# Clamped maxima go to their row in one transfer: strided query tiles, a split first hash and a new instruction list

## The chip, the cores and the metric

The kernel runs on 1 core of one Trainium2 chip. The metric is the device time of one execution in microseconds (us); lower is better. Three runs of the kernel before gave 386.69, 387.50 and 391.12 us, a median of 387.5 us.

## What is computed

Attention in which a query sees only the keys of its own hash bucket, and then a mixture-of-experts layer on the 128 best tokens of each batch. There are 4 batches of 8 heads (32 heads), 768 tokens and 64 numbers per head.

```python
def _attn_ref(q, k, v, proj):                       # q, k, v: 4 x 8 x 768 x 64; proj: 64 x 6
    q_bits = (einsum('bhsd,dk->bhsk', q, proj) > 0)   # 6 sign bits make a bucket
    k_bits = (einsum('bhsd,dk->bhsk', k, proj) > 0)
    mask = q_bucket[:, :, :, None] == k_bucket[:, :, None, :]
    scores = where(mask, scale * q @ k.T, -1e9)
    scores = scores - max(scores, axis=-1)            # one maximum for each query
    attn = exp(scores); attn = attn / (sum(attn, axis=-1) + 1e-9)
    return attn @ v

def _moe_ref(x, w_gate, w1, w2, capacity=128):      # x: 4 x 768 x 512, the heads side by side
    for b in range(4):
        top_idx = the 128 tokens with the highest x[b] @ w_gate
        xe = x[b, top_idx]; ye = relu(xe @ w1) @ w2   # w1: 512 x 1024, w2: 1024 x 512
        out[b, top_idx] = xe + sigmoid(scores[top_idx])[:, None] * ye
```

## The kernel before

**Data of a head.** For each head `h`, `A[h % 5]` is a tile of 97 partitions by 2 by 768 numbers in f16. Slot 0 holds the queries and slot 1 the keys, one column per token. Partitions 0 to 63 are the numbers of the head, 64 to 81 are rows of signs made from the hash (they push the score of a pair from different buckets far down), and partition 96 (`MROW`) holds, in slot 0, each query's clamped maximum, which the matmul with the keys' row of constants then subtracts. `Bt[h % 4]` holds the same numbers in another arrangement, with the low-order rests of the f32 inputs (`XL`), and is added in a second matmul.

**The work of a head, by the words of the list.** `X` loads queries and keys, `xh` (ScalarE) and `xl` (GpSimd) split them in f16 parts, `h` and `sg` make the signs for four heads at once, and `pa`, `ps`, `pb` are transfers that put these parts into `A` and `Bt`. Then comes a first pass for the maximum. `kd` subtracts two thirds of the keys from their neighbours; `mx.h.g.s` (`max_unit`, L538) multiplies the query tiles of a group with a third of the keys: group 0 has four query tiles of 128, group 1 has two, and there are three steps `s`, so 18 matmuls of 256 columns and 18 weight loads a head, whose stationary operand is `a[0:KM, 0, t * P : (t + 1) * P]`, tile `t` being 128 neighbouring queries. Between two steps `re` (ScalarE, L546) applies a relu in place. `rd` (VectorE, L554) reduces over the keys, which leaves `m`, 128 partitions by 6: partition `p`, column `t` is the maximum of query `t * 128 + p`.

**From the maxima to the row.** For heads 2 to 31 four words follow: `mq` (`max_clamp`, L562, VectorE) writes the clamped and scaled maxima into the first 6 columns of a tile of 128 by 128; `mt` (`max_turn`, L566, TensorE) transposes that tile into a PSUM tile; `mc` (`max_copy`, L570, VectorE) copies its 6 partitions by 128 into `mr`; and `mr` (`max_row`, L575) starts, on SyncE's queue, the transfer of `mr` to partition 96 of `A`. Heads 0 and 1 (`ROWS`) take another way (`mk`, `mu`, `mv`), with small matmuls straight to partition 96.

**After the row.** `s.h.u` (`st_unit`, L624 and L627) computes scores for five units of a head, `e` (ScalarE, L640) exponentiates, `r` (VectorE, L654) takes the rests, `a.h.c` (`av`, L708) multiplies with the values, 18 matmuls of 64 or 65 columns for a chunk of 128 keys, and `rc`, `n`, `po` divide and put out. The words `sc`, `tp`, `ty`, `ts`, `sb`, `lt`, `ow`, `cl`, `cw`, `se`, `ip`, `ix`, `ga` rank and gather the tokens of a batch, `up`, `hh`, `hl`, `dn`, `fi` are the two layers (L963, L994), and `sr` scatters the result.

**The start.** Head 0 is hashed directly from its f32 input, in two halves of 384 tokens: `hx.0.0` and `hx.0.1` (`hash_direct`, L338, TensorE) write columns 0 to 383 and 512 to 895 of one PSUM tile of 1024 columns (`big`), and `sx.0.i.e` (`signs_direct`, L349, VectorE) turns half `e` into the signs of slot `i`. `dd.0.0.0` and `da.0.1.0` (L363, L360) copy rows of the input to `A[0]`, and `da.0.0.1`, `da.0.1.1` copy them to `Bt[0]` on ScalarE. `wa.k.n` are n matmuls without use for the result.

**What sets the order.** A list of words written out by hand or by a planner (`ORDER`) is executed word by word, and each engine and each queue takes its own instructions in that order. `BANKS` gives, for each PSUM tile in the order of the list, which of four slots it takes (three of 1024 columns, one of 512). Waits between engines follow from tiles that are written and read.

Of the kernel before, what the change touches and what calls it, by code (L numbers as in the profile page):

```python
# [10 lines left out]
F16 = mybir.dt.float16  # L11
# [8 lines left out]
P = 128  # L20
# [29 lines left out]
X.5 s.0.0 mx.1.0.2 vw.0 zb ws.0 xl.3 e.0.0 wc.0 rd.1.0 mx.1.1.2 rd.1.1 s.0.2 pp xh.6 w.0 mk.1.1 ps.2.0 mk.1.0 pb.1.1  # L50
kd.2 X.4 pa.3.1 ps.3.1 e.0.2 r.0.0 s.0.1 e.0.1 r.0.1 ia.3 X.7 s.0.3 e.0.3 xh.5 vs.1 ps.3.0 mu.1.0 mv.1.0 xl.6 pb.2.3
s.0.4 V.2 a.0.0 pb.2.2 a.0.1 a.0.2 e.0.4 mu.1.1 xh.4 mx.2.1.0 mv.1.1 re.2.1.0 mx.2.0.0 pb.3.3 pa.3.0 pa.5.1 s.1.3
re.2.0.0 kd.3 mx.2.1.1 ia.4 e.1.3 a.0.3 ia.2 mx.2.0.1 re.2.0.1 re.2.1.1 s.1.4 e.1.4 r.0.2 s.1.0 e.1.0 xl.5 xh.7
mx.2.0.2 xl.4 X.8 pa.4.0 mx.2.1.2 rd.2.0 rd.2.1 mq.2 pa.4.1 a.0.4 a.0.5 s.1.2 pb.2.0 rc.0 mt.2 e.1.2 mc.2 pb.2.1
pa.5.0 X.10 n.0 s.1.1 mx.3.0.0 e.1.1 w.1 mr.2 pb.5.2 mx.3.1.0 re.3.1.0 xl.7 pb.3.0 pa.6.0 h.1.0.4 r.1.0 a.1.0 r.1.1
a.1.1 a.1.2 re.3.0.0 mx.3.0.1 a.1.3 pb.4.3 vh.1 xh.8 re.3.0.1 pb.3.2 vw.1 sg.1.0.4 r.1.2 a.1.4 vr.1 ws.1 wc.1 mx.3.1.1
a.1.5 re.3.1.1 vl.1 vs.2 xh.10 rc.1 n.1 s.2.0 e.2.0 xl.8 wt.0 mx.3.0.2 vw.2 w.2 ps.4.1 ps.4.0 ps.5.1 s.2.2 X.11
mx.3.1.2 rd.3.0 ps.5.0 rd.3.1 mq.3 e.2.2 r.2.0 s.2.1 e.2.1 s.2.3 ps.6.1 e.2.3 V.3 pb.3.1 mt.3 mc.3 s.2.4 ws.2 wc.2
e.2.4 a.2.0 pa.6.1 kd.4 mx.4.0.0 r.2.1 mr.3 X.12 ps.6.0 re.4.0.0 ps.7.0 X.9 mx.4.1.0 re.4.1.0 kd.5 pb.6.2 a.2.1 r.2.2
# [141 lines left out]
def body(ctx, tc, qk, v, pj, wg, w1, w2, cst, cst16, out):  # L201
# [84 lines left out]
    def init_rest():  # L286
# [4 lines left out]
        for i in range(2):  # L291
            nc.gpsimd.memset(wide(f"mqi{i}"), 0.0)
# [40 lines left out]
    def hash_direct(h, e):  # L333
        if e == 0:
            st["hx", h] = big(f"hx{h}")
# [728 lines left out]
```

## Time and profile before

| | us |
|---|---|
| median of 3 runs | 387.5 |
| the profiled execution | 388.95 |
| its span from first to last instruction | 387.2 |
| TensorE busy in the span | 372.9 (96%) |
| ScalarE busy | 305.1 (79%) |
| VectorE busy | 301.7 (78%) |
| GpSimd busy | 138.8 (36%) |

Busy time is the union of an engine's instructions. The matmuls of TensorE overlap in their pipeline, so that one matmul lasts longer than the interval after which the next one starts; intervals between starts tell what a matmul costs.

### The profile page before, as it was taken

Reading aid. Unit: us, or ns where it says so; the run is one execution under the profiler, and the core shown is the slowest. Engines: PE = TensorE matmul, PEld = TensorE weight load, DVE = VectorE, ACT = ScalarE, POOL = GpSimd, SP = SyncE. Lnnn points to the kernel's source line nnn. Section 1 sums busy time; section 2 is a strip of 40 time slices with the busy share of each in tenths; the row PEclk is TensorE's granted clock in tenths of the full one; section 3 lists DMA queues with packets and bytes.
Section 4 is the critical chain, followed back from the end, with each engine's and each line's share of the span. In section 5 each row is a group of like instructions: output and inputs, shape, how many; then the busy total and the mean of one; then the engine's idle time right before and its main releaser. Section 6 shows DMA issues by size and latency. Waiting matters only on the chain.

```text
span 387.2 us, 13730 instructions
## 1 busy us (share of the span) xinstructions
PE 372.9 (96%) x5730; PEld 285.5 (74%) x5730; DVE 301.7 (78%) x666; ACT 305.1 (79%) x416; POOL 138.8 (36%) x157
## 2 busy tenths in 40 slices
PE   6899998999999999999999999999999999999994
PEld 4366877776777787878788886677787788797771
DVE  3686967887879999987987977859789989767521
ACT  4699999989998899999988788887788888651110
POOL 4777567258344246255432150436010200000021
PEclk9899999999999999999999999999999999999998
DMA  7477569676674566664555545333424514002110
GB/s 214 125 217 216 168 206 266 211 190 180 180 237 145 144 169 189 176 199 154 161 172 148 175 117 160 92 83 92 97 71 117 156 48 136 2 3 84 29 56 27
DMA packets 33850, 54.33 MB, mean 140 GB/s; under 512 B 5443, under 2 KB 25137, under 8 KB 33788
## 3 DMA queue, kind: packets, MB, share of 16 engines
q1 hardware_dynamic: 32908, 50.96, 45.5%
q0 software_dynamic: 640, 2.10, 1.7%
q8 instruction: 45, 0.74, 0.8%
q10 hardware_dynamic: 240, 0.39, 0.4%
q14 instruction: 17, 0.14, 0.1%
HBM read 26.04 MB, written 7.35 MB: 86 GB/s over the span
## 4 chain that ended last, share of the span: by engine, by line
PE 77%; ACT 8%; DVE 6%; issue 5%; DMA 2%; POOLq 0%; SPq 0%; DVEq 0%; ACTq 0%
PE av L708 23%; PE s L624 14%; PE s L627 14%; PE mx L538 13%; PE hp L963 4%; PE yp L994 4%; ACT mx L546 3%; ACT P L640 3%; PE h L380 2%; DVE R L654 1%; DVE m L554 1%; DMA X<-in_qk_dram 1%; DMA out_dram<-xe,idx 1%; DVE sg L393 1%; ACT V L462 1%
## 5 line engine op out<-in xcount | busy, mean ns | idle before, releaser
L640 ACT ACTIVATE P<-s 128x1024 int32<-128x1024 f32 (+1 forms) x160 | 145.5, 942 | 22.6 <-PE s L627 21.1
L624 PE MATMUL s<-A 97*128 97x256 f16 (+1 forms) x384 | 118.4, 326 | 1.1 <-DVE mr L570 0.3
L708 PEld LDWEIGHTS <-P 128*128 128x128 f16 x2304 | 115.3, 97 | 5.5 <-issue 0.3
L708 PE MATMUL av<-V,P 128*128 128x65 f16 (+1 forms) x2304 | 119.3, 193 | 0.0
L627 PE MATMUL s<-B 128*128 128x256 f16 (+1 forms) x384 | 117.9, 326 | 0.0
L708 PE MATMUL av<-VR,R 128*128 128x65 f16 x1152 | 115.6, 192 | 0.1
L546 ACT ACTIVATE mx<-mx 128x512 f32<-128x512 f32 (+2 forms) x127 | 99.4, 802 | 16.0 <-PE mx L538 12.1
L708 PEld LDWEIGHTS <-R 128*128 128x128 f16 x1152 | 105.2, 98 | 0.2 <-DVE R L654 0.2
L654 DVE TENSOR_SCALAR R<-P 128x1536 f16<-128x1536 uint16 x96 | 94.8, 999 | 9.4 <-ACT P L640 9.3
L412 POOL TENSOR_TENSOR XL<-X,XH 128x768 f16<-128x768 f32 x31 | 50.9, 1644 | 72.2 <-DMA A<-mr 17.6
L554 DVE TENSOR_REDUCE m<-mx 128x2 f32<-128x512 f32 (+1 forms) x65 | 60.6, 952 | 15.7 <-PE mx L538 15.0
L538 PEld LDWEIGHTS <-A 82*128 82x128 f16 x570 | 50.5, 97 | 22.0 <-issue 6.6
L538 PE MATMUL mx<-kd,A 82*128 82x256 f16 (+1 forms) x378 | 59.1, 273 | 1.4 <-DVE kd L512 0.5
L627 PEld LDWEIGHTS <-B 128*128 128x128 f16 x384 | 37.6, 98 | 20.7 <-issue 2.4
L624 PEld LDWEIGHTS <-A 97*128 97x128 f16 x384 | 37.4, 97 | 19.1 <-issue 0.8
L876 POOL DMA_INDIRECT xe<-out_dram,idx x4 | 6.5, 1628 | 79.6 <-DVE idx L871 79.4
L538 PE MATMUL mx<-A 82*128 82x256 f16 (+1 forms) x192 | 31.0, 273 | 1.3 <-ACT mx L546 0.9
L401 ACT CAST XH<-X 128x768 f16<-128x768 f32 x32 | 26.7, 839 | 2.3 <-DMA X<-in_qk_dram 2.2
L483 POOL TENSOR_TENSOR vs<-Vf 128x384 f32<-128x384 f32 x16 | 16.9, 1053 | 28.6 <-DMA Vf<-in_v_dram 28.5
L963 PE MATMUL hp<-xth,w1l 128*128 128x128 f16 x128 | 22.2, 219 | 0.0
L963 PE MATMUL hp<-xtl,w1h 128*128 128x128 f16 x128 | 22.2, 219 | 0.0
L963 PE MATMUL hp<-xth,w1h 128*128 128x128 f16 x128 | 22.2, 219 | 0.0
(110 smaller groups left out, 448.1 us busy)
## 6 DMA issues: line engine op xcount, KB each, us to landing
X<-in_qk_dram SPq DMA_DIRECT2D x30, 384.0 KB
Vf<-in_v_dram SPq DMA_DIRECT2D x16, 384.0 KB
out_dram<-x SPq DMA_DIRECT2D x8, 768.0 KB
A<-XH SPq DMA_DIRECT2D x62, 96.0 KB
B<-XL SPq DMA_DIRECT2D x62, 96.0 KB
B<-A SPq DMA_DIRECT2D x62, 96.0 KB
wt<-in_w_dram SPq DMA_DIRECT2D x8, 512.0 KB
A<-sg SPq DMA_DIRECT2D x62, 27.0 KB
```

Of the source, the lines that this page charges most:

```text
L401: nc.scalar.copy(xh, st["X", h])
L412: turn(nc.gpsimd.tensor_tensor(**rest_x(h)))
L483: nc.gpsimd.tensor_tensor(y, t[:, 0:3], t[:, 3:6], op=ALU.add)
L538: nc.tensor.matmul(p[:, t - t0], a[0:KM, 0, t * P : (t + 1) * P], keys, start=first, stop=True, skip_group_check=True,)
L546: nc.scalar.activation(p, p, AF.Relu)
L554: nc.vector.reduce_max(st["m", h][:, t0:t1], max_tile(h, g), axis=AX.X)
L624: nc.tensor.matmul(p[:, o : o + n], a[:, 1, c * P : (c + 1) * P], a[:, 0, q0 : q0 + n], start=True, stop=False,)
L627: nc.tensor.matmul(p[:, o : o + n], bt[:, 1, c * P : (c + 1) * P], bt[:, 0, q0 : q0 + n], start=False, stop=True,)
L640: nc.scalar.activation(pp[:, c0 : c0 + k, q0 : q0 + w], p[:, : k * w].rearrange("p (c q) -> p c q", c=k), AF.Exp, bias=PB * float(np.log(2 ...
L654: mine(nc.vector.tensor_scalar(r, pp.bitcast(U16)[:, :, 0::2], 2.0 ** -24, None, op0=ALU.mult,))
L708: nc.tensor.matmul(o[:, t, 0:n], l, r, start=False, stop=last and l is lo, skip_group_check=True,)
L963: nc.tensor.matmul(o, l[:, k, fs], st[r, b][:, xs], start=(j == 0 and k == 0 and n == 0), stop=(k == 3 and n == 2), skip_group_check=True,)
```

## The change

The query tiles of the maximum pass are no longer 128 neighbouring queries for heads 2 to 31: tile `t` holds the queries `6 p + t`. The maximum of query `6 p + t` then stands in partition `p`, column `t`, and the 128 by 6 numbers, read partition after partition, are in the order of the row. So `max_row` moves them from the clamped tile itself to partition 96, and the transpose and the copy (`mt`, `mc`) of 30 heads go away, with 30 PSUM tiles. The stationary operand of L538 is now read with a step of 6 numbers (12 bytes) instead of 1; the tile `mq` is 128 by 6 in three buffers instead of 128 by 128 in two, and the two memsets that cleared it are gone. The two halves of the first hash write two PSUM tiles. In the list, `da.0.0.1` and `da.0.1.1` are replaced by the transfers `pb.0.0` and `pb.0.1`, `wa.1` has 10 matmuls instead of 12, and the list and the slots are otherwise made anew: 2035 words instead of 2095, 284 PSUM tiles instead of 313.

```diff
-        for i in range(2):
-            nc.gpsimd.memset(wide(f"mqi{i}"), 0.0)
...
     def hash_direct(h, e):
-        if e == 0:
-            st["hx", h] = big(f"hx{h}")
-        hp = st["hx", h]
+        hp = st["hx", h, e] = one(f"hx{h}_{e}")
         for i in range(2):
             nc.tensor.matmul(
-                hp[32 * i : 32 * i + 32, 512 * e : 512 * e + 384], pjt[:, 32 + 32 * i : 64 + 32 * i],
+                hp[32 * i : 32 * i + 32, :384], pjt[:, 32 + 32 * i : 64 + 32 * i],
...
+    def queries(h, t):
+
+        a = A[h % NA][0:KM, 0]
+        return a[:, t * P : (t + 1) * P] if h in ROWS else a.rearrange("k (p t) -> k t p", t=NC)[:, t]
...
             nc.tensor.matmul(
-                p[:, t - t0], a[0:KM, 0, t * P : (t + 1) * P], keys, start=first, stop=True, skip_group_check=True,
+                p[:, t - t0], queries(h, t), keys, start=first, stop=True, skip_group_check=True,
             )
...
     def max_clamp(h):
-        m = st["mq", h] = wide(f"mq{h}")
-        nc.vector.tensor_scalar(m[:, :NC], st["m", h], FLOOR, 1.0 / MS, op0=ALU.max, op1=ALU.mult)
-
-    def max_turn(h):
-        p = st["mt", h] = one(f"mt{h}").bitcast(F16)
-        nc.tensor.transpose(out=p[:, :P], in_=st["mq", h], identity=ident16)
-
-    def max_copy(h):
-        mr = st["mr", h] = sb.tile([NC, P], F16, tag="mr", name=f"mr{h}", bufs=2)
-        nc.vector.tensor_copy(mr, st["mt", h][:NC, :P])
+        m = st["mq", h] = sb.tile([P, NC], F16, tag="mq", name=f"mq{h}", bufs=3)
+        nc.vector.tensor_scalar(m, st["m", h], FLOOR, 1.0 / MS, op0=ALU.max, op1=ALU.mult)
 
     def max_row(h):
-        nc.sync.dma_start(A[h % NA][MROW:KA, 0, :], st["mr", h])
+        nc.sync.dma_start(A[h % NA][MROW:KA, 0, :], st["mq", h])
```

The head of the list before:

```
lp i0 wa.0.34 iv.0 x0.0 iv.1 x0.1 it hx.0.0 i1 X.1 l6 dd.0.0.0 X.2 X.3 sx.0.1.0 xh.0 xq.0.1 sx.0.0.0 hx.0.1 wa.1.12
da.0.1.0 sx.0.1.1 sx.0.0.1 xh.1 kd.0 h.0.1.2 sg.0.1.2 ia.1 xq.0.0 V.0 da.0.1.1 mx.0.0.0 re.0.0.0 mx.0.2.0 wa.2.6
```

and after:

```
i0 wa.0.34 iv.0 iv.1 lp x0.0 x0.1 it dd.0.0.0 hx.0.0 sx.0.1.0 X.1 sx.0.0.0 hx.0.1 wa.1.10 sx.0.1.1 i1 l6 X.2 sx.0.0.1
pb.0.0 h.0.1.2 xh.0 xq.0.1 da.0.1.0 kd.0 mx.0.0.0 X.3 xh.1 xl.1 xq.0.0 mx.0.2.0 wa.2.6 sg.0.1.2 re.0.0.0
```

## Rows read from the trace of the kernel before

**Rows 1.** The page, part 1: busy us, share of span, instructions.

```profile
PE 372.9 (96%) x5730; PEld 285.5 (74%) x5730; DVE 301.7 (78%) x666; ACT 305.1 (79%) x416; POOL 138.8 (36%) x157
```

**Rows 2.** Stretches: length, busy us by engine (instructions), granted clock, DMA share, GB/s.

```profile
4.40:8.80 4.40, 2.48 (x17) 0.71 (x17) 2.16 (x4) 3.08 (x4) 1.64 (x1) 1.00 0.90 281
8.90:12.20 3.30, 3.30 (x11) 0.91 (x9) 1.39 (x4) 0.15 (x1) 1.83 (x2) 0.50 0.57 168
...
20.80:60.00 39.20, 38.23 (x556) 28.50 (x555) 30.33 (x55) 38.37 (x54) 25.51 (x25) 1.00 0.69 203
...
200.00:345.00 145.00, 144.74 (x2357) 113.89 (x2354) 118.09 (x282) 116.77 (x160) 31.65 (x35) 1.00 0.37 103
```

**Rows 3.** Waits of TensorE and its loads: total us, times, longest us.

```profile
PE hx L338 <- DVE A L349: 1.9, 1, 1.9
PE mt L566 <- DVE mq L562: 1.4, 2, 1.0
PE s L624 <- DVE mr L570: 0.3, 1, 0.3
...
PEld L566 <- DVE mq L562: 2.8, 6, 1.3
```

**Rows 4.** Timeline of the start: start us, us, engine, line, operation, idle before.

```profile
5.04 0.69 PE L338 MATMUL hx<-X,pjt 128*32 128x384 f32 x2
...
5.65 0.55 DVE L363 CAST A<-X 64x768 f16<-64x768 f32 x1 [5.65 <-DMA X<-in_qk_dram]
...
6.24 1.36 DVE L349 TENSOR_SCALAR A<-hx,pjt 18x384 f16<-18x384 f32 x2
...
7.36 0.83 ACT L401 CAST XH<-X 128x768 f16<-128x768 f32 x1
...
7.65 0.84 PE L338 MATMUL hx<-X,pjt 128*32 128x384 f32 x4 [1.92 <-DVE A L349]
...
8.22 0.83 ACT L360 CAST B<-X 64x768 f16<-64x768 f32 x1
...
8.42 0.98 PE L667 MATMUL av<-ones 128*128 128x116 f16 x12
...
9.33 2.77 PE L380 MATMUL h<-X,pjt 128*32 128x384 f32 x4
...
9.94 0.35 DVE L512 TENSOR_TENSOR kd<-A 82x384 f16<-82x384 f16 x1
...
12.03 0.43 PE L538 MATMUL mx<-kd,A 82*128 82x384 f16 x1
```

**Rows 5.** The chain that ended last: start us, us, what (matmuls).

```profile
46.78 0.06 PE mt L566
...
331.93 0.06 PE mt L566
```

**Rows 6.** Groups by line: busy us, mean ns, idle before and its releaser.

```profile
L570 DVE COPY mr<-mt 6x128 f16<-6x128 f16 x30 | 6.2, 207 | 6.6 <-PE mt L566 6.3
```

**Rows 7.** The same chain, pieces of one kind of matmul.

```profile
47.95 0.66 PE mx L538 x6
...
59.56 1.63 PE av L708 x54
...
196.33 0.67 PE hp L963 x12
```

**Rows 8.** Timeline of TensorE: a score matmul and the maximum pass behind it.

```profile
151.54 0.38 PE L627 MATMUL s<-B 128*128 128x512 f16 x1
151.75 0.60 PE L538 MATMUL mx<-A 82*128 82x256 f16 x4
```

**Rows 9.** Timeline of SyncE's queue and TensorE: head 25's row and scores.

```profile
275.65 0.76 SPq L575 DMA_DIRECT2D A<-mr  x1
...
279.14 0.38 PE L624 MATMUL s<-A 97*128 97x512 f16 x1
```

**Rows 10.** The page, part 3: packets, MB, share of 16 engines.

```profile
q1 hardware_dynamic: 32908, 50.96, 45.5%
```

More of the change, by code (lines that the diff above doesn't have):

```diff
@@ L50 @@
[L50 to L59, printed above, removed]
@@ new lines @@
+xh.3 ps.1.0 pa.2.0 kd.1 vh.0 h.0.2.4 mk.0.0 mx.1.1.0 re.1.1.0 mx.1.0.0 re.1.0.0 vs.0 mu.0.0 sg.0.2.4 mv.0.0 mx.1.1.1
+re.1.1.1 mk.0.1 vl.0 mx.1.0.1 vr.0 re.1.0.1 vw.0 X.6 ia.1 s.0.0 xl.3 e.0.0 mu.0.1 mx.1.0.2 mv.0.1 rd.1.0 zb ws.0
+pa.2.1 pb.1.0 xh.6 mx.1.1.2 wc.0 w.0 rd.1.1 s.0.2 V.1 ps.2.0 xl.6 mk.1.1 mk.1.0 e.0.2 s.0.1 e.0.1 s.0.3 s.0.4 e.0.3
+ps.2.1 kd.2 mx.2.0.0 re.2.0.0 mx.2.1.0 re.2.1.0 r.0.0 a.0.0 a.0.1 X.5 pb.1.1 mu.1.0 pp e.0.4 pb.1.3 xh.5 r.0.1
+mx.2.0.1 a.0.2 re.2.0.1 vs.1 pb.1.2 X.4 mv.1.0 xh.4 r.0.2 mu.1.1 mv.1.1 s.1.3 e.1.3 xl.5 xl.4 ps.3.0 pa.3.1 a.0.3
@@ new lines @@
+a.7.4 mx.10.0.1 X.21 pb.10.1 kd.11 e.8.1 a.7.5 rc.7 n.7 ws.5 re.10.0.1 wl.3.0 s.9.0 wl.3.1 wc.5 mx.10.0.2 rd.10.0
+xl.17 s.8.3 pa.12.0 e.9.0 vh.5 mx.10.1.0 re.10.1.0 h.3.0.4 vl.5 sc.0.1.0 w.8 pb.11.1 s.8.4 e.8.3 a.8.0 sg.3.0.4
+mx.10.1.1 sc.0.1.3 s.9.2 wt.4 e.8.4 V.7 r.8.2 sc.0.1.5 r.8.1 mx.11.0.0 re.10.1.1 s.9.1 sc.0.1.4 mx.10.1.2 e.9.2
+re.11.0.0 pa.12.1 mx.11.1.0 rd.10.1 a.8.1 a.8.2 vw.6 e.9.1 sc.0.1.1 pa.13.1 mx.11.0.1 re.11.0.1 mq.10 a.8.3 a.8.4
+re.11.1.0 sc.0.1.2 tp.0 ps.13.1 a.8.5 r.9.0 mx.11.0.2 po.1 mr.10 ps.12.1 ty.0 wh.4 ts.0 mx.11.1.1 re.11.1.1 vs.7 rc.8
@@ new lines @@
+s.12.2 e.12.2 r.12.0 mr.13 X.23 s.12.1 e.12.1 r.12.1 a.11.3 mx.14.0.0 re.14.0.0 mx.14.1.0 re.14.1.0 kd.15 a.11.4
+a.11.5 mx.14.0.1 ga.0 xh.21 re.14.0.1 rc.11 h.4.0.4 n.11 pb.15.3 vh.7 s.12.3 e.12.3 pb.15.2 po.2 vs.8 mx.14.1.1
+sg.4.0.4 sc.1.0.0 wl.5.1 mx.14.0.2 rd.14.0 ps.16.1 sc.1.0.3 w.12 s.13.0 s.12.4 ps.17.1 ps.16.0 re.14.1.1 xl.21 e.12.4
+pa.17.0 a.12.0 vr.7 r.12.2 gt.0 s.13.2 pb.16.3 e.13.0 mx.14.1.2 pb.16.2 rd.14.1 wt.6 e.13.2 s.13.1 mx.15.0.0 ps.17.0
+pa.17.1 xh.22 re.15.0.0 a.12.1 mx.15.1.0 a.12.2 a.12.3 r.13.0 mx.15.0.1 e.13.1 r.13.1 pb.14.1 ge.0 a.12.4 a.12.5
@@ new lines @@
+wh.7 ws.9 wl.7.1 h.5.0.4 sg.5.0.4 re.18.0.0 mx.18.0.1 pa.20.0 e.16.1 a.15.3 mx.18.1.0 re.18.1.0 vs.10 pb.18.0
+re.18.0.1 vw.10 a.15.4 a.15.5 ps.20.1 wc.9 rc.15 n.15 sc.1.1.0 r.16.1 sc.1.1.2 mx.18.1.1 re.18.1.1 s.17.0 pb.19.2
+ps.20.0 kd.19 mx.18.0.2 pb.19.3 e.17.0 rd.18.0 mx.18.1.2 w.16 s.16.4 s.16.3 vh.9 e.16.3 a.16.0 po.3 a.16.1 ps.21.1
+rd.18.1 a.16.2 e.16.4 s.17.2 e.17.2 mx.19.1.0 re.19.1.0 wl.7.0 vl.9 a.16.3 sc.1.1.5 sc.1.1.4 r.16.2 s.17.1 mx.19.0.0
+re.19.0.0 up.0.0 up.0.1 e.17.1 mx.19.0.1 re.19.0.1 sc.1.1.3 pb.20.3 mq.18 vr.9 a.16.4 a.16.5 pb.20.1 sc.1.1.1 kd.20
@@ L172 @@
+up.3.6 hl.3.0 dn.3.0 up.3.7 dn.3.1 hh.3.1 dn.3.2 dn.3.3 hl.3.1 dn.3.4 dn.3.5 sr.1 dn.3.6 dn.3.7 sr.2 fi.3 sr.3
 """
 BANKS = """
[4 rows of a table removed]
[3 rows of a table added]
 """
@@ L582, in clamp_part @@
         t = part(g)
-        m = st["mq", h, g] = wide(f"mq{h}_{g}")
+        m = st["mq", h, g] = sb.tile([P, NC], F16, tag="mq", name=f"mq{h}_{g}", bufs=3)
         nc.vector.tensor_scalar(m[:, t], st["m", h][:, t], FLOOR, 1.0 / MS, op0=ALU.max, op1=ALU.mult)
```

226 lines of the change are left out of this document (104 added, 122 removed), and 7 rows, old and new, of the table BANKS.

## The prediction

> **What bounds the kernel now.** I read the page's busy times first: TensorE is busy for 96% of the span, the other engines for less than 80% [rows 1]. Since matmuls overlap, that alone proves little, so I cut the span in stretches. From 200 to 345 us TensorE is busy 144.74 of 145 us; from 20.8 to 60 us it and ScalarE are both at 98%; in the start, from 4.4 to 8.8 us, TensorE does 2.48 us of work in 4.4 [rows 2]. So there are a start that waits, a first third in which ScalarE is as full as TensorE, and a rest that TensorE sets alone. The last matmul ends at 381.9 us of 387.2, so TensorE's queue runs the length of the kernel. Third, I listed what TensorE waits for. The longest wait is the first hash's second half on VectorE, 1.9 us; the next is the transpose `mt` on the clamp `mq`, 1.4 us in 2 waits; its weight loads wait 2.8 us in 6 [rows 3]. Fourth, in the chain that ended last the reader sees the transposes as pieces of 0.06 us: 25 of the 30 lie on it, 23 at 0.06 and two longer ones, the first and the last of which are shown [rows 5].
>
> **Part by part.** *The split hash.* `hx.0.1` starts at 7.65 us after 1.92 us of waiting, and what releases it is VectorE's reading of the other half of the same PSUM tile [rows 3, 4]. Its input was there: the copy of the whole row of head 0 began at 5.65 us, when the transfer landed, and TensorE was through with the first half at 5.04 + 0.69 = 5.73 us [rows 4]. With a tile of its own it starts at 5.73. Then come its own 0.77 us (7.65 to 8.42), 10 matmuls without use at 0.91 / 12 = 0.076 us each (8.42 to 9.33), so `h.0.1.2` at 7.26, or at 7.36, when ScalarE read its input, head 1's [rows 4]. It took 2.70 us (9.33 to 12.03) in a stretch whose granted clock was 0.50, the 1.2 GHz level, behind 4.4 us in which TensorE was busy 2.48 [rows 2, 4]. At that clock it ends at 10.1; at full clock it would take half, to 8.7. The maximum pass also needs `kd.0`, behind four sign instructions of 1.36 / 2 = 0.68 us each from 6.24 on: 8.96 + 0.35 = 9.3 us, where it ended at 10.3 [rows 4]. So `mx.0.0.0` starts between 9.3 and 10.1 instead of 12.03: 1.9 to 2.7 us earlier. I take **2.0**, near the end that keeps the clock as the row has it. Until head 0's scores the same chain follows; I shift it whole. The low end is 0, if a later load or ScalarE takes it back.
>
> *The transfers to `Bt[0]`.* Two ScalarE copies of 0.83 us each go [rows 4]; between 0 and 1.7 us, and I take 0, as they run beside TensorE's wait for other things. On SyncE's queue `pb.0.0` waits for `dd.0.0.0` (6.2 us), and `X.3`, `ia.0` and `pa.1.1` are queued behind it, `X.3` by some 2 us; its first reader, `h.0.2.4`, comes after the whole maximum pass of head 0. Cost 0 under that cover; without it, those 2 us.
>
> *The transposes.* 30 x 0.06 us = **1.8** off TensorE's queue [rows 5]. Their waits, 1.4 us at TensorE and at most the 2.8 us of the loads [rows 3], go too: nothing on TensorE waits for `mq` any more, only SyncE's queue. What is late next there is the relu or the reduction of the same head, so between 0 and 2.8; I take **1.4**, the one that TensorE itself shows.
>
> *The copies* `mc` take 6.2 us off VectorE [rows 6], which is 78% busy and off the path except where `mt` waited: 0, and nothing below. *PSUM:* 30 tiles fewer and one more. No row names a wait for a slot, so I take 0, and up to 1 us of gain as an estimate. *The memsets:* GpSimd, 0, idle beside.
>
> *The strided loads.* 540 weight loads (30 heads x 18) now step 12 bytes. No row has this step. The nearest is the weight load from `P` in `av`, whose f16 halves of 32-bit words step 4 bytes: those chunks of matmuls go at 1.63 / 54 = 0.030 us each, loads included [rows 7], while a matmul of the maximum pass occupies 0.66 / 6 = 0.11 us [rows 7]. So a load may be 3.6 times slower than in `av` and still be hidden. Exposed first is the load of a unit that directly follows `av` work, of which the new list has 58: the matmul ahead covers 0.03 us only. From both sides: 0, and 58 x (0.11 - 0.03) = 4.6 us if a load took as long as the matmul it should hide behind. I take 0, by the `av` row.
>
> The Trainium skill, "SBUF — State Buffer", section "Door 1: The DMA port swizzle", says that SBUF lines are 16 bytes and that at least two reads must hit a line for full bandwidth. By that a 12-byte step (1.3 numbers a line) pays a penalty that a 4-byte step (4 a line) does not; the page gives no size, and the sum by it would lie between mine and the 4.6 us above.
>
> *The row's transfer.* 128 pieces of 12 bytes from 128 partitions in place of 6 of 256. A packet of this queue took 0.455 x 16 x 387.2 / 32908 = 0.086 us on average [rows 10]; 128 over 16 engines are 8 each, so at most 0.7 us more to the landing as an estimate. Cover: head 25's row was issued 3.49 us before its scores began [rows 9], and all heads together show one wait of 0.3 us for the row [rows 3]. From the clamp to a head's first score unit the new list has at least 4.8 us of TensorE work (heads 2 and 26; median 6.5), counted by its words at 0.22 us for a 512-column score matmul [rows 8], 0.11, 0.03 and 0.056 for the others [rows 7]. 0.2 for the clamp, 3.5 for the row and 0.7 make 4.4. Cost 0.
>
> *The new list.* I compared its TensorE work between dependent words with the old one's: the distances from clamp to scores are about the same. Between -1.5 and +2 us as an estimate from the 1.1 and 1.4 us of single waits; I take 0.
>
> **Sum:** 2.0 + 1.8 + 1.4 = 5.2 us. From the profiled execution (388.95, of which 387.2 is span) it gives 383.75; that execution stands 1.45 above the median, and the same 5.2 from 387.5 gives **382.3**.
>
> **The rivals.**
> (a) *The waits come back.* In the first 100 us ScalarE is as full as TensorE [rows 2], so what the start and the transposes free is spent waiting for ScalarE's relu. For it: the chain passes through ScalarE there. Against: from 200 us on TensorE is alone. Then the 1.8 us of the transposes alone stay: 385.7. Chance 0.20.
> (b) *The strided loads show* behind `av`: 382.3 + 4.6 = 386.9. Against it stands the `av` row, at a third of the step; for it, that no row has 12 bytes. Chance 0.06. The line rule of the Trainium skill, "SBUF — State Buffer", cited above, is what would bring it about.
> (c) *Slower: the row comes late.* Scores of head `h` wait at L624 for the pieces. Summed over the 30 heads by the distances counted above, a chain of 6.0 us from clamp to landing costs 7.3 us (11 heads short), one of 6.5 us 13.9 us (15 heads): 389.6 to 396.2. It decides from about 6 us; the known chain is 4.4. Chance 0.08. The Trainium skill, "DMA: Bandwidth & Descriptors", section "Rules for kernel authors", warns against transposing with a plain DMA of a rearranged access pattern (19 times slower than the hardware's transpose); 12-byte pieces come near that; no row here shows such a transfer.
> (d) *The new list is worse* by more than all gains: 0.04 slower.
> (e) *The hash isn't released* by two tiles, because something else ends the wait at 7.65: 382.3 + 2.0 = 384.3. Chance 0.05.
>
> **How the numbers follow.** A measurement of this kernel can tell about 1% from no change: 383.6 and 391.4 us. The forecast and its better neighbours hold 0.57, and all of that is faster; (a), (b) and (e) lie within 1%, 0.20 + 0.06 + 0.05 = 0.31; (c) and (d) 0.12. The low end, 379.5, takes 2.7 for the start, the 2.8 us of load waits and half a us from ScalarE's copies and the slots; the high end, 388, reaches over (a), (b) and (e) and 1 us on, and leaves out (c) and (d).
>
> **What would show it.** Right: `hx.0.1` near 5.7 and `mx.0.0.0` before 10.2 us; head 0's scores near 18.8 us instead of 20.8; no L566; no TensorE wait for the row beyond a few tenths; the intervals of L538 still 0.11 us, also behind `av`. Wrong: idle TensorE time before L624 released by the row's transfer, L538 intervals over 0.11, or more TensorE waits for L546 in the first 100 us.

## The result and the profile after

The changed kernel takes **384.34 us** (median of 4 runs, 383.69 to 386.47), the kernel before on the same chip 387.68 (4 runs): a ratio of 0.9897, interval 0.9852 to 0.9942. The forecast was 382.3, its range 379.5 to 388.0. Two later measurements gave 386.61 against 388.98 (0.9932, 0.9901 to 0.9963) and 385.37 against 388.66 (0.9901, 0.9866 to 0.9936). So the change is worth 2.6 to 4.0 us. In us the three intervals are 2.2 to 5.7, 1.4 to 3.8 and 2.5 to 5.2: the forecast's 5.2 is inside the first, outside the second and at the end of the third, so it was most likely too many. Four of the kernels below had one run each that took over 1.5% longer than that kernel's fastest; it is left out of ranges, ratios and counts of runs, not of medians.

The profiled execution took 386.47 us, 384.7 of which is span. The page's busy line answers to [rows 1]: 32 weight loads fewer (the 30 transposes and two matmuls without use; six more matmuls are only missing from this trace, c_after has 5698 of both), 1.1 us less of TensorE, and a span 2.5 us shorter.

```profile
PE 371.8 (97%) x5692; PEld 292.9 (76%) x5698; DVE 296.3 (77%) x636; ACT 303.2 (79%) x414; POOL 139.7 (36%) x155
...
q1 hardware_dynamic: 37028, 51.16, 48.1%
```

The timeline of the start (start us, us, engine, line, operation, idle before), against [rows 4]:

```profile
5.54 0.55 DVE L355 CAST A<-X 64x768 f16<-64x768 f32 x1 [5.54 <-DMA X<-in_qk_dram]
...
5.58 0.84 PE L330 MATMUL hx<-X,pjt 128*32 128x384 f32 x4 [0.51 <-DMA X<-in_qk_dram]
6.12 2.76 DVE L341 TENSOR_SCALAR A<-hx,pjt 18x384 f16<-18x384 f32 x4
...
7.01 1.48 PE L372 MATMUL h<-X,pjt 128*32 128x384 f32 x4
...
8.91 0.35 DVE L504 TENSOR_TENSOR kd<-A 82x384 f16<-82x384 f16 x1
...
9.32 0.48 PE L535 MATMUL mx<-kd,A 82*128 82x384 f16 x2 [0.83 <-DVE kd L504]
```

`hx.0.1` starts at 5.58 us, not 7.65, and what releases it is its input. `h.0.1.2` takes 1.48 us, where it took 2.70. `kd.0` and the maximum pass come at 8.91 and 9.32; head 0's scores start at 18.48 us, where they started at 20.82.

TensorE's waits (total us, times, longest), against [rows 3]:

```profile
PE mx L535 <- DVE kd L504: 1.8, 2, 1.0
PE mx L535 <- ACT mx L543: 1.8, 4, 0.5
PE av L653 <- POOL V L295: 1.0, 1, 1.0
PE rp L826 <- DVE cm L805: 0.7, 2, 0.4
PE tp L785 <- ACT mx L543: 0.5, 1, 0.5
PE hx L330 <- DMA X<-in_qk_dram: 0.5, 1, 0.5
PE s L610 <- DVE sg L385: 0.4, 1, 0.4
```

Three lines of the same view of before, which [rows 3] leaves out:

```profile
PE mx L538 <- ACT mx L546: 1.1, 3, 0.7
...
PE mx L538 <- DVE kd L512: 0.5, 1, 0.5
...
PE s L624 <- ACT P L640: 0.2, 1, 0.2
```

The waits for the hash's other half and for the clamp are gone, and no line names the row's transfer (`A<-mq`). The maximum pass waits more: 1.8 us for `kd`, which was 0.5, and 1.8 for ScalarE's relu, which was 1.1. Both waits for `kd`, and all of the relu's but 0.5 us, lie before 18 us, in heads that never had a transpose.

Stretches of the same trace (length, busy us by engine with instructions in brackets, granted clock, DMA share, GB/s), against [rows 2]:

```profile
4.40:12.30 7.90, 6.30 (x46) 2.92 (x43) 5.67 (x9) 4.95 (x7) 4.45 (x3) 1.00 0.81 241
12.30:17.65 5.35, 3.35 (x22) 1.40 (x22) 4.94 (x6) 3.49 (x6) 4.65 (x7) 1.00 0.71 188
17.65:24.48 6.83, 6.81 (x28) 3.70 (x28) 4.51 (x10) 4.08 (x7) 3.87 (x3) 0.50 0.72 225
24.48:60.00 35.52, 35.45 (x549) 28.02 (x548) 26.96 (x47) 35.03 (x48) 22.25 (x23) 1.00 0.73 201
```

The clock stays at its upper level through the start, where it had been 0.50 at 8.90 to 12.20 us, and is 0.50 (the 1.2 GHz level) at 17.65 to 24.48 us instead, behind a stretch in which TensorE is busy 3.35 of 5.35 us.

The best single view of where the time went is the start of each head's first score matmul, read from the timelines, less its start in the profile of before (us; one profiled execution each; the second column is the time at which VectorE's copy of head 0's input starts, when the input has landed):

| kernel | input landed | head 0 | 1 | 4 | 8 | 16 | 27 | 28 | 31 |
|---|---|---|---|---|---|---|---|---|---|
| changed, first profile | 5.54 | -2.34 | +0.89 | -2.20 | -2.94 | -1.97 | -2.61 | -2.80 | -3.13 |
| changed, second profile (c_after) | 4.58 | -2.90 | -1.59 | -4.67 | -5.40 | -4.82 | -5.46 | -2.94 | -3.27 |
| changed and filled (e6_fill) | 4.67 | -2.87 | -1.56 | -3.91 | -3.87 | -2.71 | -3.35 | -3.04 | -3.37 |
| changed and filled (e6_fill_2) | 5.62 | -2.62 | -1.31 | -3.44 | -3.22 | -2.87 | -3.52 | -3.71 | -4.03 |
| split alone, old list (e1_split) | 4.98 | -3.12 | -3.12 | -3.12 | -2.78 | -2.02 | -2.32 | -2.33 | -2.34 |
| row alone, old list (e4_row_old_list) | 5.98 | +0.32 | +0.35 | +0.27 | -0.22 | -0.47 | -0.87 | -0.83 | -0.92 |
| row, transposes kept (e5_idle_turns) | 6.26 | +0.57 | +0.59 | +0.66 | +0.65 | +0.71 | +0.88 | +0.93 | +1.00 |
| both, old list (e9_both_old_list) | 6.10 | -1.99 | -1.96 | -2.03 | -2.53 | -2.80 | -2.99 | -2.95 | -3.04 |

Such a difference carries the luck of two executions: head 0's input landed at 5.65 us in the profile of before, and up to 1.07 us earlier or 0.61 later in the others, which moves a whole row of the table with it.

### The profile page after: what moved, and what is told of

Read it like the earlier page. It is cut to its first block, busy times and chain, and to the rows that moved or that the text cites. A ratio compares the mean times of both kernels' runs of the same rounds, so it can differ in the third digit from the quotient of the medians.

```text
span 384.7 us, 13626 instructions
## 1 busy us (share of the span) xinstructions
PE 371.8 (97%) x5692; PEld 292.9 (76%) x5698; DVE 296.3 (77%) x636; ACT 303.2 (79%) x414; POOL 139.7 (36%) x155
## 3 DMA queue, kind: packets, MB, share of 16 engines
q1 hardware_dynamic: 37028, 51.16, 48.1%
## 4 chain that ended last, share of the span: by engine, by line
PE 77%; DVE 8%; ACT 6%; issue 5%; DMA 2%; POOLq 0%; SPq 0%; ACTq 0%; DVEq 0%
PE av L694 23%; PE s L610 15%; PE s L613 14%; PE mx L535 14%; PE hp L949 4%; PE yp L980 3%; ACT mx L543 3%; ACT P L626 2%; PE h L372 2%; DVE cm L805 1%; DVE co L816 1%; DVE R L640 1%; DMA X<-in_qk_dram 1%; ACT XH L393 1%; DVE kd L504 1%
## 5 line engine op out<-in xcount | busy, mean ns | idle before, releaser
L626 ACT ACTIVATE P<-s 128x1024 int32<-128x1024 f32 (+1 forms) x160 | 145.7, 944 | 18.7 <-PE s L613 17.3
L543 ACT ACTIVATE mx<-mx 128x512 f32<-128x512 f32 (+2 forms) x127 | 99.3, 804 | 17.9 <-PE mx L535 16.5
L640 DVE TENSOR_SCALAR R<-P 128x1536 f16<-128x1536 uint16 x96 | 96.6, 1015 | 14.0 <-ACT P L626 12.3
L535 PEld LDWEIGHTS <-A 82*128 82x128 f16 x570 | 60.1, 126 | 17.3 <-issue 7.4
L535 PE MATMUL mx<-kd,A 82*128 82x256 f16 (+1 forms) x378 | 60.7, 277 | 2.9 <-DVE kd L504 1.8
L475 POOL TENSOR_TENSOR vs<-Vf 128x384 f32<-128x384 f32 x16 | 18.7, 1171 | 46.7 <-DMA Vf<-in_v_dram 46.6
L862 POOL DMA_INDIRECT xe<-out_dram,idx x4 | 5.1, 1269 | 64.5 <-DVE idx L857 64.4
L704 DVE TENSOR_SCALAR rc<-av 128x6 f32<-128x6 f32 x32 | 5.2, 162 | 24.6 <-PE av L694 23.3
```

The lines of the kernel that those rows point to most:

```text
L475: nc.gpsimd.tensor_tensor(y, t[:, 0:3], t[:, 3:6], op=ALU.add)
L535: nc.tensor.matmul(p[:, t - t0], queries(h, t), keys, start=first, stop=True, skip_group_check=True,)
L543: nc.scalar.activation(p, p, AF.Relu)
L626: nc.scalar.activation(pp[:, c0 : c0 + k, q0 : q0 + w], p[:, : k * w].rearrange("p (c q) -> p c q", c=k), AF.Exp, bias=PB * float(np.log(2 ...
L640: mine(nc.vector.tensor_scalar(r, pp.bitcast(U16)[:, :, 0::2], 2.0 ** -24, None, op0=ALU.mult,))
```

## The experiments

Each kernel ran beside the kernel before, in three sets: e1_split, e2_joined, e4_row_old_list and e5_idle_turns (before: 388.26 us, 35 runs); c_after, e6_fill, e9_both_old_list and e10_two_hops (388.98, 23 runs); c_after_2, e6_fill_2, e12_old_fill and e13_pool_hop (388.66, 15 runs). A ratio is turned into us by its set's median.

**e1_split**: the kernel before and its list, with the two tiles of the first hash alone.

```diff
-        if e == 0:
-            st["hx", h] = big(f"hx{h}")
-        hp = st["hx", h]
+        hp = st["hx", h, e] = one(f"hx{h}_{e}")
```

> The kernel before, old list, with one thing changed: the two halves of the first hash write two PSUM tiles (the second takes the slot of 512 columns). Theory (the start is worth about 2 us, the transposes the rest): the second half starts near 5.7 us instead of 7.65, head 0's scores about 2 us earlier, and the time is 385.7 us against 387.7. Rival (the start is given back, since ScalarE or a lower granted clock takes it): the hash starts early, but the time stays at 387.7 within 0.5.

Measured: 386.49 us (12 runs, 385.26 to 387.91), 0.9956 (0.993 to 0.9981), so -1.7 us (-0.7 to -2.7). In its profile the clock is 1.00 from 4.4 to 60 us, and head 0's scores come 3.12 us earlier, 0.67 of which is an earlier landing of the input. None of its 12 runs has a mean clock under 0.996, where 13 of the 35 of the kernel before have, so a part of the gain is the clock that is kept. By head 16 only 2.02 us of the 3.12 are left (the table), and 2.34 at head 31. Most of that goes between the scores of heads 8 and 10, where TensorE waits 0.24 us for a row and 0.71 for the clamp, against 0.33 for the clamp before. The hash's wait was real; a part of what it frees is lost again in the first third.

**e2_joined**: the changed kernel, its new list too, with the first hash in one tile again (the edit above, reversed).

> The changed kernel with its new list, but with the two halves of the first hash in one PSUM tile of 1024 columns again. Theory: the second half waits for VectorE once more, head 0's scores come about 2 us later, and the time is 386.3 us against 384.3 for the changed kernel. Rival (start given back): 384.3 within 0.5.

Measured: 387.93 us (12 runs), 0.9968 (0.9936 to 1.0), so -1.2 us (0 to -2.5). In its profile the wait is back:

```profile
PE mx L537 <- ACT mx L545: 2.5, 5, 0.7
PE hx L332 <- DVE A L343: 1.5, 1, 1.5
...
PE s L612 <- DMA A<-mq: 0.9, 1, 0.9
```

Against the changed kernel's -2.6 to -4.0 us the split is worth 1.4 to 2.8 in the new list, by ratios whose intervals overlap or touch. `h.0.1.2` took 1.48 us here although TensorE had waited: the low clock behind that wait, which begins at 8.2 to 8.9 us in the profiles of before, e4_row_old_list and e5_idle_turns, did not come here; the clock fell at 17.9 us, as in after. Counted from the landing of the input (4.65 us here), head 0's scores start 13.7 us later, against 12.9 in after and 13.4 in c_after; by these profiles the split brings less here than in the old list.

**e4_row_old_list**: the old list with `mt` and `mc` struck, every sixth query, the clamp's [128, 6] tile moved directly, the hash in one tile.

```diff
-                p[:, t - t0], a[0:KM, 0, t * P : (t + 1) * P], keys, ...
+                p[:, t - t0], queries(h, t), keys, ...
...
-        nc.sync.dma_start(A[h % NA][MROW:KA, 0, :], st["mr", h])
+        nc.sync.dma_start(A[h % NA][MROW:KA, 0, :], st["mq", h])
```

> The kernel before with its old list, from which only the words of the transposes and copies are taken out, with strided query tiles and the row moved straight from the clamped tile. The first hash keeps its one tile. Theory: 1.8 us of transposes and 1.4 us of their waits go, 0.8 us of strided loads behind the value matmuls (58 times 13 ns, from the profile of the changed kernel) come: 2.4 us less, 385.3 against 387.7. Rival 1 (the waits come back as waits for ScalarE): 1.0 less, 386.7. Rival 2 (it is the new list that brings the gain): 387.7 or more.

Measured: 387.83 us (12 runs), 0.998 (0.9948 to 1.0011), so -0.8 us (+0.4 to -2.0). TensorE's waits in its profile:

```profile
PE mx L538 <- ACT mx L546: 1.7, 6, 0.7
...
PE s L624 <- DVE sg L388: 0.9, 1, 0.9
PE s L624 <- ACT P L640: 0.8, 2, 0.6
```

No wait for `mq` is left, as forecast. But the relu, which made TensorE wait 1.1 us in 3 before, now makes it wait 1.7 in 6, and the scores wait 1.7 us in 3 for signs and exponents, where they had waited 0.2. The longest wait for the clamp in before, and then what stands in that place here, from the timelines of TensorE:

```profile
66.87 0.23 PE L566 MATMUL mt<-c,mq 128*128 128x128 f16 x1 [1.04 <-DVE mq L562]
```

```profile
58.01 0.38 PE L624 MATMUL s<-A 97*128 97x512 f16 x1 [0.61 <-ACT P L640]
...
66.79 0.38 PE L538 MATMUL mx<-kd,A 82*128 82x256 f16 x2 [0.23 <-ACT mx L546]
...
68.11 0.38 PE L624 MATMUL s<-A 97*128 97x512 f16 x1 [0.94 <-DVE sg L388]
```

The stretch from head 0's first scores to head 31's, where all kernels of the old list do the same work but for the row, shows the sum: length and TensorE's busy time of before, of this kernel, of e5_idle_turns and of e9_both_old_list below (each in its own trace):

```profile
20.82:337.33 316.51, 312.93 (x4993) 243.47 (x4991) 266.01 (x582) 281.50 (x383) 123.28 (x124) 1.00 0.54 154
```

```profile
21.13:336.42 315.29, 311.70 (x4961) 249.99 (x4962) 261.60 (x552) 281.10 (x383) 125.80 (x124) 1.00 0.55 155
```

```profile
21.39:338.33 316.94, 313.73 (x4991) 251.38 (x4991) 265.79 (x582) 281.56 (x383) 125.76 (x124) 1.00 0.56 154
```

```profile
18.83:334.30 315.47, 311.85 (x4964) 249.98 (x4962) 261.59 (x552) 281.06 (x383) 125.92 (x124) 1.00 0.56 155
```

TensorE's idle time there is 3.58 us before, 3.59 here and 3.62 in e9_both_old_list: without the transposes it waits as long as with them, for others. What is gained is busy time, 1.23 us here. The time, 387.83, is what the second rival said; its reason, that the new list brings the gain, falls with e9_both_old_list below.

**e5_idle_turns**: the same in the old list, but the transposes and their copies stay in as work that nobody reads.

```diff
-        nc.sync.dma_start(A[h % NA][MROW:KA, 0, :], st["mr", h])
+        nc.sync.dma_start(A[h % NA][MROW:KA, 0, :], st["mq", h][:, :NC])
```

> As the run with the old list and the direct row, but the 30 transposes and copies stay in as work that nobody reads. So against the kernel before it has only the strided loads and the direct transfer. Theory: 0.8 us more for the loads, 388.5 against 387.7, and 3.2 us above the run without transposes. Rival (the row's shorter way is what helps, not TensorE's 30 instructions): about the time of the run without transposes, 385.3.

Measured: 389.65 us (12 runs), 1.0032 (1.0003 to 1.006), so +1.2 us (0.1 to 2.3): the strided loads and the small pieces cost something once nothing is gained for them. From head 0 to head 31 it falls behind by 1.00 - 0.57 = 0.43 us, and e4_row_old_list moves ahead by 0.92 + 0.32 = 1.24. Of the 0.43, TensorE's busy time is +0.80 (313.73 against 312.93) and its idle time -0.37, one wait for the clamp less. Between this kernel and e4_row_old_list lie 1.67 us, and 2.03 of busy time: the transposes' own 30 x 0.056 = 1.7 us, a little more, and nothing of their waits. By the ratios the two kernels are 2.0 us apart, where 3.2 were expected.

**c_after** and **c_after_2**: the changed kernel unaltered, in the second and the last set.

> The changed kernel itself, unaltered, as the measure for the three beside it on one chip. By the first measurement (384.34 us median of 4 runs, 383.69 to 386.47) I expect 384 to 385 us, 3 to 4 us under the kernel before. The spread is part of the question: if the low granted clock that the profile showed from 17.65 to 24.48 us comes and goes from run to run and is worth up to 2.2 us, runs with a mean clock under 0.992 are 1.5 to 2.5 us longer than those over 0.997; if it is regained later as before (3.2 us lost, 2.2 to 2.9 regained by head 8), the two kinds differ by under 1 us.

> The changed kernel unaltered, once more, as the measure for the three beside it, and for a second profile of where the granted clock falls. From 12 runs on one chip (386.61 us median against 388.98 before, runs with a mean clock of 0.996 or more at 385.2, the others at 386.96) I expect a ratio of 0.990 to 0.996 again, and a gap of 1.5 to 2.5 us between runs with and without a low stretch of the clock. Rival: the gap was chance, and the two kinds lie within 0.7 us.

Measured: 386.61 us (12 runs, 383.74 to 388.4) and 385.37 (383.5 to 387.2), the ratios above. The first lies over the 384 to 385 us that I expected. With the first measurement these are 21 runs of the changed kernel. Divided at a mean granted clock of 0.996, a bound that I drew after seeing the first of the sets, 12 of them have a median of 384.76 us and 9 of 386.96, a gap of 2.2 us. The mean clock does not tell all: the fastest run of c_after, 383.74 us, has 0.992. The kernel before splits less: at 0.996 or more it takes 388.72 us in the set of c_after and 387.78 in that of c_after_2, where the changed kernel at such a clock takes 385.2 and 384.53 (medians of 4 to 12 runs). So among runs that kept the clock the change is worth 3.5 and 3.3 us: the clock explains the spread, and not why 5.2 was too many. The profile of c_after_2 (390.15 us) has the low stretch in the start again, from 17.3 us on, and one wait of 2.3 us for the relu at 90 us; so the start lost its clock in two of the changed kernel's three profiles.

The start in c_after kept its clock:

```profile
12.30:17.65 5.35, 3.51 (x24) 1.54 (x24) 4.91 (x7) 3.48 (x6) 4.47 (x7) 1.00 0.73 208
17.65:24.48 6.83, 6.38 (x44) 3.93 (x43) 6.18 (x10) 6.38 (x9) 5.12 (x4) 1.00 0.72 212
```

Its profile (386.34 us, mean clock 0.996) shows a loss late. Its stretches around 296 us:

```profile
292.00:294.00 2.00, 2.00 (x38) 1.52 (x36) 2.00 (x5) 1.63 (x3) 1.81 (x3) 1.00 0.46 104
294.00:296.00 2.00, 0.95 (x10) 0.49 (x8) 1.93 (x8) 1.08 (x2) 0.81 (x3) 0.99 0.45 124
296.00:299.20 3.20, 3.20 (x28) 2.10 (x27) 3.07 (x10) 2.16 (x3) 0.00 (x0) 0.50 0.60 202
```

and the timeline of VectorE and TensorE there:

```profile
292.11 2.14 DVE L816 SCALAR_TENSOR_TENSOR co<-sbc,sc,cs 128x128 bf16<-128x128 f32 x3
...
295.16 0.18 PE L826 MATMUL rp<-oneb,co 128*128 128x1 bf16 x1 [0.70 <-DVE co L816]
295.69 0.23 PE L826 MATMUL rp<-oneb,cm 128*128 128x1 bf16 x3 [0.35 <-DVE cm L805]
```

Until head 27 this execution was 5.46 us ahead, a little more than the forecast, 1.07 of it by an earlier landing of the input. Then TensorE waited 1.05 us for two of VectorE's counts, the clock was at its lower level for the next 3.2 us, and at head 28 it was 2.94 ahead. The three `co` took 2.14 us here, with GpSimd busy for 1.98 of the 2.20 us around them, and 1.65 in e6_fill, with GpSimd busy for 1.09 of 1.70; that GpSimd slowed them is possible, and was not tried.

**e6_fill**: the changed kernel with 42 more matmuls without use in the start.

```diff
-h.0.1.2 ... wa.2.6 ... wa.3.8 ... h.0.2.4
+h.0.1.2 wa.4.14 ... wa.2.10 ... wa.3.16 ... h.0.2.4 wa.5.16
```

> The changed kernel with 42 more matmuls without use in the start (14 behind h.0.1.2, 4 and 8 more in the two groups that stand there, 16 behind h.0.2.4), so that TensorE has fewer gaps between 8.5 and 17.6 us. Theory: the granted clock of 0.50 from 17.65 to 24.48 us in the profile of the changed kernel comes from the gaps before it (TensorE busy 6.06 of 8.8 us there), and part of it stays in the time: with the gaps filled no stretch under 0.9 is left behind 12 us, every run's mean clock is at least 0.997, and the median falls by 0.5 to 1.5 us against the changed kernel on the same chip. First rival: the gaps were needed as slack, and 42 x 0.03 to 0.08 us of matmuls push the start back: slower by 0.5 to 2 us. Second rival: what the low clock costs is regained behind head 4 in any case, where ScalarE sets the pace: the mean clock rises, the median stays within 0.5 us.

> The changed kernel with 42 more matmuls without use in the start, once more (384.74 us in 6 runs, all at a mean clock of 0.997 or more, beside 386.61 of the changed kernel). Theory: the fill keeps the clock from falling in the start, so again no run under 0.996, and a median 1 to 2 us under the changed kernel's on the same chip. Rival: the first 6 runs were a lucky draw; the median is within 0.7 us of the changed kernel's, with some runs under 0.996.

Measured: 384.74 us (6 runs), 0.9896 (0.9859 to 0.9932), and 385.04 (6 runs), 0.9894 (0.9868 to 0.992). All 12 runs have a mean clock of at least 0.997, where 9 of the changed kernel's 21 are under 0.996. The first profile, against the stretches of after shown above:

```profile
4.40:12.30 7.90, 7.35 (x68) 4.05 (x68) 5.61 (x9) 4.89 (x7) 4.95 (x4) 1.00 0.83 247
12.30:17.65 5.35, 4.71 (x49) 2.66 (x47) 4.78 (x9) 3.71 (x6) 4.19 (x6) 1.00 0.62 169
17.65:24.48 6.83, 6.38 (x44) 3.93 (x43) 6.00 (x9) 6.40 (x9) 5.10 (x4) 1.00 0.79 245
```

The first part of the theory held: no run under a mean clock of 0.997 in either set. The second held in part: the median is 1.9 us under the changed kernel's in one set and 0.3 in the other, and the intervals overlap. What is clear is that the worst runs are gone: 383.84 to 386.24 us, where the changed kernel has 383.5 to 388.4. Its ratio to the kernel before is the lowest in either set. The fill explains only the drop in the start; c_after kept its clock there with 3.51 us busy of the 5.35, and fell at 296 us.

**e9_both_old_list**: split and row together in the old list, from which only `mt` and `mc` are struck (the edits of e1_split and e4_row_old_list).

> The kernel before with the split hash and the direct row with every sixth query, but in the old list, from which only the transposes and their copies are struck. It is the change without its new list. My prediction took 0 for the new list, so it expects the time of the changed kernel, within 1 us: 384 to 385 us. The rival reads the two halves measured alone in the old list, -1.8 us (split hash) and -0.4 us (row), as additive: 385.8 to 386.3 us, and the new list by itself would then be worth 1.3 to 2 us.

Measured: 386.04 us, 0.9923 (0.9897 to 0.9948), so -3.0 us (-2.0 to -4.0), beside -2.6 of the changed kernel in the same set. The two halves alone add up to -1.7 - 0.8 = -2.5. So the parts add within intervals of 1 us, and the new list by itself (with the transfers to `Bt[0]`, which this kernel does not have) brings nothing that these intervals show. The table shows why it could look otherwise: c_after is 2.9 us ahead of this kernel at head 8, 1.5 of it by its input, which landed earlier, and level with it at head 28.

**e12_old_fill**: the last kernel with the fill of e6_fill.

> Both parts of the change in the old list (386.04 us beside 388.98 before), with the same 42 matmuls without use behind the same words. In the old list only 3 of 11 runs had a mean clock under 0.996, and those cost 0.4 us; so if the clock is what the fill mends, it brings little here: within 0.7 us of 386.0. Rival: the fill helps by something else than the clock, and brings 1 to 2 us here too, to 384.0 to 385.0.

Measured: 387.19 us (385.83 to 388.57), 0.9956 (0.9933 to 0.998): 1.3 us worse than e9_both_old_list by the two ratios, and neither theory said so. Only 3 of e9_both_old_list's 11 runs are under a mean clock of 0.996, so the fill had little to save. In its profile it is ahead of e9_both_old_list at head 8 (-2.86 against -2.53) and behind at head 10 (-1.92 against -2.70): between them TensorE waits 0.39 us for a row and 0.71 for ScalarE's relu, where e9_both_old_list waits 0.18. e1_split, which was as far ahead, loses 0.8 us in the same place. How much of the 1.3 us that explains was not followed further.

**e10_two_hops**: the changed kernel with each head's row moved through a tile of one row, both transfers on SyncE's queue.

```diff
-        nc.sync.dma_start(A[h % NA][MROW:KA, 0, :], st["mq", h])
+        rw = sb.tile([1, S], F16, tag="rw", name=f"rw{h}", bufs=1)
+        nc.sync.dma_start(rw, st["mq", h])
+        nc.sync.dma_start(A[h % NA][MROW:KA, 0, :], rw)
```

> The changed kernel, but each head's row goes from the clamp to one row of a small tile first, and from there to its place: two transfers in place of one, the second issued on the same queue when the first has landed. That lengthens the chain from the clamp to the scores by some 2 to 2.5 us, to about 6 us or more by the trace (issue 0.5 us, landing 1.6 to 3.1 us after it, twice). My prediction put the price of a chain of 6.0 us at 7.3 us and of 6.5 us at 13.9 us, by the distances in the list: 391 to 398 us, with waits of TensorE for the row at most heads. Rival: the list's distances are shorter than the time that really passes between clamp and scores, since other work fills in and TensorE's waits move; then the second hop costs 0 to 2 us. What SyncE's queue has behind the waiting second transfer (head loads) moves back by about 2 us too, which would add to either.

Measured: 422.22 us (6 runs), 1.0846 (1.079 to 1.0902), +33 us, far above either theory. The page's busy line, the waits of SyncE's queue and those of TensorE:

```profile
PE 383.7 (91%) x5698; PEld 297.1 (70%) x5698; DVE 297.2 (70%) x636; ACT 304.4 (72%) x414; POOL 139.3 (33%) x155
```

```profile
SPq L563 <- DMA rw<-mq: 70.3, 30, 4.4
...
PE s L612 <- DMA A<-rw: 17.2, 8, 4.3
...
PE mx L535 <- DMA A<-sg: 2.2, 1, 2.2
PE mx L535 <- DMA A<-rw: 1.7, 1, 1.7
...
PE s L615 <- DMA B<-A: 1.4, 1, 1.4
```

This run measures two things. One hop lands 70.3 / 30 = 2.3 us after the end of its issue. And the span grew by 35.0 us, of which 383.7 - 372.9 = 10.8 are a TensorE that is busy longer for nearly the same work (its clock averages 0.966; five stretches at 0.50 between 52 and 227 us last 27.3 us together) and 38.5 - 14.3 = 24.2 idle time: some 19 of it for rows, some for loads that stood behind the waiting transfer.

**e13_pool_hop**: the same, with the second transfer issued by GpSimd.

```diff
-        nc.sync.dma_start(A[h % NA][MROW:KA, 0, :], rw)
+        nc.gpsimd.dma_start(A[h % NA][MROW:KA, 0, :], rw)
```

> The row in two hops as before, but the second transfer is issued by GpSimd, so that SyncE's queue no longer stands behind the landing of the first (70.3 us of such waits in 30, with all head loads behind them). The chain from clamp to landing stays at about 6 us or more. Theory A (the queue was the cost): 388 to 396 us, as my count of distances has it for a chain of 6.0 to 6.5 us, and TensorE's waits for the row fall from 18.9 to 4 to 12 us. Theory B (the longer chain by itself cost 35 us): 410 to 425 us again, with row waits near 19 us. GpSimd's own casts are held up by the 30 waits instead; if that decides, the waits are for loads that follow its casts and not for the row.

Measured: 406.88 us (5 runs from 406.05 to 408.2), 1.0468 (1.0437 to 1.05), +18 us, between the theories. In its profile TensorE waits 15.5 us for rows in 10 waits, more than the 4 to 12 of theory A, and SyncE's queue still waits 13.3 us in 7 for the second hop to have read the one buffer of `rw`. SyncE's queue was a good part of e10_two_hops, but not all, and the edit did not free it wholly. How much of the rest is the longer chain, how much that one buffer and how much GpSimd, which now waits for the landings, stays open.

## Why the prediction was right and wrong

**The split hash: right, and larger at first than taken.** `hx.0.1` at 5.58 us (5.73 forecast), the maximum pass at 9.32 (9.3 to 10.1). I kept the low clock for `h.0.1.2`, as the row of before had it, and took 2.0 of a possible 2.7. With the wait gone the clock did not fall there, and head 0 came 2.0 to 3.1 us earlier in the kernels of the table with the split. Counted from the landing of the input the luck drops out: `hx.0.1` starts 2.0 us later in all four kernels with one tile, and head 0's scores 15.1 to 15.2 us later in the three of them with the old list, against 12.7 in e1_split and e9_both_old_list, so 2.4 us earlier. "I shift it whole" is the weak step: e1_split has given back 1.1 us by head 16. By its runs the split is worth 1.7 (0.7 to 2.7), which does not rule out 2.0. Rival (e) is out.

**The transposes' own time: right.** 1.8 forecast; 2.0 us of TensorE's busy time between e4_row_old_list and e5_idle_turns.

**Their waits: wrong, and this is the step that failed.** "I take 1.4, the one that TensorE itself shows." The waits for `mq` did go, but in e4_row_old_list TensorE waits for relu, signs and exponents instead, 3.4 us where these had been 1.3, and its idle time from head 0's to head 31's scores is 3.58 us before, 3.59 and 3.62 without the transposes: 0 in place of 1.4. That is one profile of each kernel, in the old list; the changed kernel is idle for 2.5 us in that stretch in after, 3.3 in c_after, 4.5 in e6_fill and 3.7 in e6_fill_2, on both sides of it. Rival (a) described it, priced against the whole sum: with the 1.4 left out, the forecast is 383.7. The working said that the next to be late was the relu, and still took the gain in full. The range, 379.5 to 388.0, reached over (a) as well, so that the time lies in it tells nothing on this step.

**The strided loads: 0 was too low by 0.8 us.** Loads of the maximum pass take longer. First the line of the page of before, then that of after (line, engine, operation, tiles, count, busy us, mean ns, idle before):

```profile
L538 PEld LDWEIGHTS <-A 82*128 82x128 f16 x570 | 50.5, 97 | 22.0 <-issue 6.6
```

```profile
L535 PEld LDWEIGHTS <-A 82*128 82x128 f16 x570 | 60.1, 126 | 17.3 <-issue 7.4
```

From 97 to 126 ns on the mean, and nearly all of it lies behind matmuls that occupy 109 ns; the intervals between those did not change. The one place that shows is what the forecast named: the first interval of a unit that follows `av` goes from 112 ns in the old list to 125 in the 58 places of the new one (from the starts of TensorE's matmuls in both traces), 0.75 us in all; in e5_idle_turns TensorE's busy time grows by 0.80. Rival (b) had the right place and a sixth of its 4.6 us. The rule of the Trainium skill, "SBUF — State Buffer", section "Door 1: The DMA port swizzle", on reads per 16-byte line pointed the right way: the 12-byte step does cost, 1.3 times here. That the line is the reason is not shown; no other step was tried.

**The row's transfer: right, with little room.** The forecast's chain of 4.4 us is, by the first hop of e10_two_hops, 0.2 + 0.5 + 2.3 = 3.0 when the queue is free; in after the clamp's start to the end of the issue takes 0.7 us at the median and 4.2 at the longest. TensorE's waits name the row in no line of after or of c_after, but once each, with 0.4 to 0.9 us, in e2_joined, e6_fill, e6_fill_2 and e12_old_fill. Rival (c) did not happen. Its price for a longer chain, 7.3 us at 6.0 and 13.9 at 6.5, was not put to the test at those lengths. In e10_two_hops the clamp to the end of the second issue takes 5.7 us at the median, so some 8 us to the landing by the first hop's 2.3, and it costs 33 us; in e13_pool_hop the clamp to the landing takes 6.8 us at the median of its profile, and it costs 18. More than the length is in both: in e10_two_hops the second transfer holds up what is behind it on the queue, and TensorE was at its lower clock for 27.3 us; in e13_pool_hop there are the one buffer of `rw` and GpSimd's part.

**The new list: 0, as taken,** by e9_both_old_list beside c_after. What no step of the forecast had is the clock behind new gaps: the first profile of the changed kernel is 0.56 us behind c_after at head 0 (its input landed 0.96 later), 2.48 at head 1, behind the stretch at 0.50, and still 2.85 at head 27.

The sum as measured: 1.7 for the split (runs of e1_split), 2.0 for the transposes and 0 for their waits, less 0.8 for the loads (TensorE's busy and idle time in single profiles) is 2.9, beside 3.0 of e9_both_old_list; the changed kernel's three measurements, 2.6 to 4.0, lie around it. This sum mixes runs and profiles, and by runs alone each part has an interval of 1 us or more to either side: 1.7 for the split and 0.8 for the row.

Of the forecast's signs of being right most came. Two of its signs of being wrong came too: intervals of the maximum pass over 0.11 us behind `av`, and more waits for the relu in the first 100 us (1.8 us against 1.1 in after).

## What to carry to other kernels

A wait that you remove is worth its time only if nothing else ends just behind it: list who is late next in that stretch, and where an engine is as full as the one you relieve, count the work taken off and not the waits. Read a gain head by head along the trace and not at its end alone: here an execution was 5.4 us ahead for most of its length and lost half of it to two waits and the low clock behind them. Read also when the first input landed before you compare two executions: here that alone moved a profile by up to 1.7 us. Do not put a transfer that must wait for another into a queue that other loads stand behind: here that came with 33 us, and 18 when the second transfer left that queue.

## What the runs showed of the hardware

- A short wait of TensorE can cost more than itself: in c_after 1.05 us of waits at 294 to 296 us were followed by 3.2 us at a granted clock of 0.50. But a stretch of much the same gaps kept the clock in one execution (3.51 of 5.35 us busy) and lost it in another (3.35 us); the kernel with 4.71 busy there had no run with a mean clock under 0.997.
- 128 pieces of 12 bytes landed 2.3 us after the end of their issue on the mean (longest 4.4, in e10_two_hops), and the issue on SyncE took about 0.5 us, where six pieces of 256 bytes took 0.76 [rows 9]; so in the timeline of after:

```profile
283.39 0.51 SPq L561 DMA_DIRECT2D A<-mq  x1
```

The queue's packets went from 32,908 [rows 10] to 37,028 without a wait of TensorE for a row in after.

- TensorE's writing of one half of a PSUM tile waited 1.9 us for VectorE's reading of the other half [rows 3]; with two tiles it did not. The program makes this wait, tile by tile; no run shows whether the memory itself would need it.
